# An attention kernel's routing chain: fewer steps for each pair of heads, the written order kept to the last pair, the lists made after it

## The chip, the cores and the metric

One core of a Trainium2 chip runs the whole program. The metric is the device time of one execution in microseconds (us). The engines are named as in the profile: PE (TensorE, matmuls), PEld (its weight loads), DVE (VectorE), ACT (ScalarE), POOL (GpSimd), SP (the queue that issues most DMAs).

## The reference

```python
# attention: B=2, H=8, S=768, D=64, 4 sink keys, window 128
scores = np.where(is_sink | in_window, (q @ k.T) / 8, -1e9)
a = softmax(scores);  x = (a @ v)            # x: 1536 tokens x 512
# first mixture: 8 experts, the best 2 of each token
logits = x @ w_gate;  ns = np.log1p(np.exp(x @ w_noise))
top2 = the two largest of (logits + ns * noise); w = softmax of these two
out[token] += w[k] * (relu(x @ w1[e]) @ w2[e])      # F = 1024
# second mixture: 8 other experts, the best one of each token, gates by softmax
```

## The kernel before

**Attention.** The 1536 tokens are 12 tiles of 128 (`t` = 0 to 11); tiles 0 to 5 are the first batch, 6 to 11 the second. A unit of work is a pair of heads of one tile; there are 48 pairs, and `for j in range(END)` (line 1040) walks over them and 9 steps beyond, which drain what is in flight. In step `j`, pair `j` gets its scores on PE (`s_mm`, line 406: 12 matmuls, or 6 in the first tile of a batch), pair `j-1` its maxima on DVE (`maxima`, lines 412 and 417), pair `j-2` its exponentials on ACT (line 425), pair `j-3` its transposes on PE (line 431), and pair `j-7` its product with v on PE (`pv`, line 461, f32). The scores have two PSUM buffers (`s`). Finished tiles are normalised (`fin_x`, line 537), split into two f16 halves (`x_split`, `x_low`), written to `xrow` in DRAM, turned (`x_turn`), and multiplied with the gate's weights (`lg_mm`, line 568). For tile 5, the last of the first group, `x_turn` is eight PE transposes into a buffer of `s` and one ACT copy (lines 562 and 563), in step 37 together with its `lg_mm`; the logits are ready in step 38.

**The two groups and the gate's chain.** `cuts` puts tiles 0 to 5 in group 0 and 6 to 11 in group 1. When the last logits of a group are there, `gate_ops` makes a list of some 70 small operations, nearly all on DVE (line 609 is the helper that issues them): the noise scale, the best two experts, their counts (PE, lines 647 to 650), ranks, then `lo` and `ct`, the two big comparisons of 128x1536 and 128x1152 elements, the product `ct * tok1`, the matmuls `place` that put the tokens in lists (line 702), and for group 0 `ahead`, which gathers the rows of the first 128 tokens of experts 0 and 1 (POOL, line 936) and queues `ahead_steps`: both layers of these two blocks (lines 894, 799, 817, 909), 28 jobs of PE work that run before group 1's list is known.

**What sets the order.** The list is dripped into the program between other work: `DR` operations after each of the three DVE steps of `maxima`, one after each of the two of `fin_x`, and `TI` at the end of a step (`TD` from step 48 on). A `BAR` in the list lets nothing pass until the end of the step:

```python
def tick(n):
    drip(n)
    for c in chains:
        if c and c[0] is BAR:
            c.pop(0)
```

Up to step `MC` each engine runs its instructions in the order in which they are written (`tc.manual_schedule`). From there on a planner orders them by its own costs, with the written order as priority, except POOL's last part and the last stage. With `MC` 29, steps 29 to 47 of the pairs are the planner's. With `DR` 3 and `TI` 20 group 0's list stands in steps 38 to 47: 29 operations in step 39, `lo`, `ct` and the product in 45, `place` in 46, the gather in 47. Steps 50 and later each issue a job, if there is one.

**After it.** While jobs or lists are left, a loop issues one job and four list operations per turn; group 1's list begins at step 62. Then the rest of experts 0 and 1, experts 2 to 7, and the second mixture follow. The second mixture's routing and experts aren't touched.

The weights of each expert come as f32 and are split into two f16 halves by ACT (line 115, and 111 where POOL makes the low half) and DVE or POOL (lines 122, 120), at written steps as well.

Of the kernel before, what the change touches and what calls it, by code (L numbers as in the profile page):

```python
# [1 line left out]
PRM = {"cuts": [0, 6, 12], "CP": 0, "BARS": 1, "DR": 3, "TI": 20, "TD": 30, "GW": 4, "JB": 50, "JN": 1, "TK": 4,  # L2
# [3 lines left out]
       "JP": 0, "XP": 0, "ptev": 5, "parts": 6, "max": 1, "finx": 10, "ptmm": 3, "exps": 2, "finsum": 9, "pv": 7,  # L6
# [33 lines left out]
def attention_moe_moe(ctx, tc, qk, v, n_sink, window, small, w1, w2, modality_id, modality_bias, w1b, w2b, out, CAP=416):  # L40
# [25 lines left out]

    cuts = PRM['cuts']
    AHEAD = 2
# [271 lines left out]
    def split(t):  # L340
        QZ[t] = qz[t % 3]
        KH[t] = khz[t % 4]
        if t < PRM['direct']:

# [6 lines left out]
        for z, o in ((0, QH[t]), (1, KH[t])):  # L351
            if PRM['qb' if z == 0 else 'kb'] >> t & 1:
                V.tensor_copy(o[:, 0], QK[t][:, z])
# [3 lines left out]
    def split_low(t, x=None):  # L357
        if t < PRM['direct']:
            for y in range(2):
                r = slice(y * D, y * D + D)  # L360
                (G if y else V).tensor_tensor(QZ[t][r, 1, y], QK[t][r, 0], QZ[t][r, 0, y], op=OP.subtract)
        elif not x:
            (V if t == 1 or PRM['ql'] >> t & 1 else G).tensor_tensor(QH[t][:, 1], QK[t][:, 0], QH[t][:, 0], op=OP.subtract)
            for y in range(2):
                r = slice(y * D, y * D + D)
                S.dma_start(QZ[t][r, :, y], QH[t][r])
        if x != 0:
            (G if PRM['kl'] >> t & 1 else V).tensor_tensor(KH[t][:, 1], QK[t][:, 1], KH[t][:, 0], op=OP.subtract)

# [204 lines left out]
    def gate_ops(gi, ts, l):  # L574
# [31 lines left out]
        def op(f, *a, **kw):  # L606
            def run():
                with tc.high_priority(offset=CP):
                    f(*a, **kw)  # L609
            ops.append(run)  # L610

        def bar(k_=1):
            if BARS:
                ops.extend([BAR] * k_)
# [77 lines left out]
        def each(x, m):  # L692
            return x.rearrange("p c k -> p (c k)")[:, None, :].to_broadcast([128, m, 2 * n])

        op(V.tensor_tensor, lo, steps2[:, :, 0:2 * n], each(rh[:, 0], 128), op=OP.is_equal)
        op(V.tensor_tensor, ct, steps2[:, 0:NCOL, 0:2 * n], each(rh[:, 1], NCOL), op=OP.is_equal)
        op(V.tensor_tensor, ct, ct, each(tok1[:, t0:t0 + n], NCOL), op=OP.mult)
        bar()

# [229 lines left out]
    CP = PRM['CP']  # L929
    BARS = PRM['BARS']  # L930
    DR, TI = PRM['DR'], PRM['TI']
# [16 lines left out]
    groups = [list(range(a, b)) for a, b in zip(cuts, cuts[1:])]  # L948

    ends = [ts[-1] for ts in groups]  # L950
    for gi, ts in enumerate(groups):
        for c, t in enumerate(ts):
            def lg(t, c, ts, gi):
                if c == 0:
                    LG[gi] = gk.tile([128, len(ts), 2 * E], FT, name=f"lg{gi}", bufs=1)
                lg_ev(t, LG[gi], c)
                if c == len(ts) - 1:
                    gate_ops(gi, ts, LG[gi][:, 0:len(ts)])
            put(4 * t + (PRM['lge'] if t in ends else PRM['lg']), lg, t, c, ts, gi)
# [68 lines left out]
    JN = PRM['JN']  # L1028
# [10 lines left out]
    MC = PRM['MC']  # L1039
# [345 lines left out]
    TK = PRM['TK']  # L1385
# [349 lines left out]
```

## Time and profile before

| what | us |
|---|---|
| median of 3 runs | 638.49 |
| the three runs | 632.25, 640.03, 638.49 |
| profiled execution, its own time | 641.03 |
| span of the profiled execution | 639.3 |
| mean granted clock over the span | 0.936 of full speed |

The profiled execution is the one that all rows below come from. A granted clock of 0.50 is TensorE at 1.2 GHz, one of 1.00 is 2.4 GHz. In the rows, PE's busy time counts a matmul as long as the profile thinks that it ran, so a PE that is busy all the time at 0.50 does half of what it would do at 1.00.

### The profile page before, as it was taken

Reading aid. Unit: us, or ns where it says so; the run is one execution under the profiler, and the core shown is the slowest. Engines: PE = TensorE matmul, PEld = TensorE weight load, DVE = VectorE, ACT = ScalarE, POOL = GpSimd, SP = SyncE. Lnnn points to the kernel's source line nnn. Section 1 sums busy time; section 2 is a strip of 40 time slices with the busy share of each in tenths; the row PEclk is TensorE's granted clock in tenths of the full one; section 3 lists DMA queues with packets and bytes.
Section 4 is the critical chain, followed back from the end, with each engine's and each line's share of the span. In section 5 each row is a group of like instructions: output and inputs, shape, how many; then the busy total and the mean of one; then the engine's idle time right before and its main releaser. Section 6 shows DMA issues by size and latency. Waiting matters only on the chain. (4 is left out here: it accounts for less than half of the span.)

```text
span 639.3 us, 13126 instructions
## 1 busy us (share of the span) xinstructions
PE 584.5 (91%) x4764; PEld 407.5 (64%) x4764; DVE 378.7 (59%) x1036; ACT 301.8 (47%) x656; POOL 247.3 (39%) x274
## 2 busy tenths in 40 slices
PE   5699989799989999999999999999999697989982
PEld 4699888688867765555555555555545573755761
DVE  8799957934835848464747563356686572473420
ACT  6469857743234847454647463233452341452210
POOL 6577754432141354243341606042312381262210
PEclk9789968857899999999999999999999899889988
DMA  6778975447028578477584506017619865489320
GB/s 211 226 227 218 268 213 149 102 133 246 19 81 210 207 237 261 124 248 175 177 247 166 124 3 154 9 59 277 194 69 338 249 157 134 149 275 215 105 66 9
DMA packets 101048, 107.61 MB, mean 168 GB/s; under 512 B 62579, under 2 KB 65939, under 8 KB 100950
## 3 DMA queue, kind: packets, MB, share of 16 engines
q1 hardware_dynamic: 90102, 76.06, 42.9%
q0 software_dynamic: 9792, 28.26, 13.1%
q10 hardware_dynamic: 1056, 2.10, 0.9%
q8 instruction: 47, 0.77, 0.5%
q14 instruction: 51, 0.42, 0.2%
HBM read 76.03 MB, written 14.74 MB: 142 GB/s over the span
## 5 line engine op out<-in xcount | busy, mean ns | idle before, releaser
L799 PEld LDWEIGHTS <-w1s 128*128 128x128 f16 x1632 | 149.5, 102 | 85.6 <-issue 17.3
L799 PE MATMUL pp<-xtt,w1s 128*128 128x416 f16 (+2 forms) x864 | 152.3, 332 | 1.8 <-issue 1.0
L817 PE MATMUL pp<-hh,w2s 128*128 128x416 f16 (+2 forms) x960 | 141.4, 307 | 0.7 <-DVE hh L802 0.6
L817 PEld LDWEIGHTS <-w2s 128*128 128x128 f16 x960 | 87.7, 99 | 50.1 <-issue 1.0
L751 POOL DMA_INDIRECT yrow<-xga,ids x34 | 36.7, 1079 | 123.7 <-ACT xga L876 118.7
L825 DVE SCALAR_TENSOR_TENSOR yt<-pp,yt 64x416 f16<-64x416 f32 (+1 forms) x64 | 35.5, 555 | 65.2 <-ACT yt L823 58.4
L801 ACT ACTIVATE hh<-pp 128x416 f16<-128x416 f32 (+3 forms) x87 | 38.5, 461 | 57.8 <-PE pp L799 50.5
L802 DVE SCALAR_TENSOR_TENSOR hh<-pp,hh 128x416 f16<-128x416 f32 (+3 forms) x87 | 44.4, 518 | 32.3 <-ACT hh L801 22.7
L823 ACT ACTIVATE yt<-pp 64x416 f16<-64x416 f32 (+1 forms) x64 | 31.0, 485 | 68.1 <-PE pp L817 61.4
L122 DVE SCALAR_TENSOR_TENSOR w1s<-wf,w1s 128x1024 f16<-128x1024 f32 (+1 forms) x49 | 54.3, 1119 | 13.5 <-ACT w1s L115 10.0
L1539 PEld LDWEIGHTS <-hh 128*128 128x128 f16 x336 | 32.6, 98 | 37.9
L122 DVE SCALAR_TENSOR_TENSOR w2s<-wf,w2s 128x1024 f16<-128x1024 f32 (+1 forms) x43 | 52.6, 1262 | 3.3 <-ACT w2s L115 2.8
L461 PE MATMUL po<-vf,ptm 128*128 128x65 f32 x320 | 53.1, 319 | 0.6 <-issue 0.4
L1539 PE MATMUL po<-w2s,hh 128*128 128x512 f16 x240 | 52.8, 379 | 0.0
L461 PEld LDWEIGHTS po<-vf,ptm 128*128 128x128 f32 x320 | 51.2, 241 | 1.9 <-issue 1.2
L115 ACT ACTIVATE w1s<-wf 128x1024 f16<-128x1024 f32 (+1 forms) x51 | 45.6, 924 | 10.6 <-DMA wf<-in_moe_w_dram 5.0
L406 PEld LDWEIGHTS <-w2s 128*128 128x128 f16 x528 | 39.2, 113 | 14.2 <-issue 6.0
L115 ACT ACTIVATE w2s<-wf 128x1024 f16<-128x1024 f32 (+1 forms) x52 | 46.4, 918 | 0.9 <-remote 0.6
L763 POOL DMA_INDIRECT xg<-xrow,idg x30 | 30.2, 1008 | 29.0 <-DVE dst L609 20.1
L802 DVE SCALAR_TENSOR_TENSOR hh<-ph,hh 128x256 f16<-128x256 f32 (+1 forms) x48 | 17.2, 377 | 38.7 <-ACT hh L801 35.8
L406 PE MATMUL s<-w1s,w2s 128*128 128x128 f16 x264 | 31.4, 258 | 7.7 <-DVE w1s L348 5.4
L801 ACT ACTIVATE hh<-ph 128x256 f16<-128x256 f32 (+1 forms) x48 | 15.7, 347 | 46.7 <-PE ph L799 43.4
(304 smaller groups left out, 832.2 us busy)
## 6 DMA issues: line engine op xcount, KB each, us to landing
wf<-in_moe_w_dram SPq DMA_DIRECT2D x44, 1024.0 KB
w1s<-in_qk_dram SPq DMA_DIRECT2D x12, 512.0 KB
vf<-in_v_dram SPq DMA_DIRECT2D x12, 260.0 KB
xrow<-xr SPq DMA_DIRECT2D x12, 256.0 KB
w2s<-xga SPq DMA_DIRECT2D x22, 128.0 KB
wf<-in_moe_w_dram ACTq DMA_DIRECT2D x2, 1024.0 KB
yrow<-xga,ids POOLq DMA_INDIRECT x34
xtt<-xg SPq DMA_TRANSPOSE x31
```

What stands on the lines that cost most here:

```text
L115: A.activation(t[:, 0][:, o[0], o[1]], i, AF.Copy, scale=1.0 if v else SW)
L122: V.scalar_tensor_tensor(t[:, 1][:, o[0], o[1]], i, SW, h, op0=OP.mult, op1=OP.subtract)
L406: T.matmul(PS[t, p][:, c, j], head(t, a, 2 * p + j), KH[t - c][:, b, p // 2 * 2 + j], start=(j + a + b + c == 0), stop=(a > 0 and c == n - ...
L461: T.matmul(o[:, 2 * pp + j], x[:, 2 * pp + j], VV[t - c][:, 2 * p + j], start=(pp + j + c == 0), stop=(i == 0 and j + pp == 2), skip_group ...
L751: return G.indirect_dma_start(out=dst, out_offset=bass.IndirectOffsetOnAxis(ap=idx, axis=0), in_=src, in_offset=None, bounds_check=n - 1, ...
L799: ordered(1, T.matmul(p[:, :n], wa[:, a, d, fs], x[:, c * KD + d, r], start=(k_ == 0), stop=(k_ == len(passes) - 1)))
L801: A.activation(hh[:, 0, f, q], p[:, :n], AF.Relu)
L802: V.scalar_tensor_tensor(hh[:, 1, f, q], p[:, :n], 0.0, hh[:, 0, f, q], op0=OP.max, op1=OP.subtract)
L817: ordered(2, T.matmul(p[:, :n], wt[:, a, f, dd], hh[:, c, f, q], start=(k_ == 0), stop=(k_ == len(passes) - 1)))
L823: A.activation(y[s, 2 * d + x, r], p[s, :n], AF.Copy, scale=z)
L825: V.scalar_tensor_tensor(y[hs[1 - x], 2 * d + x, r], p[s, :n], z, y[s, 2 * d + x, r], op0=OP.mult, op1=OP.subtract)
L1539: T.matmul(p[:m], hh[:, c, f, o:o + m], wb[:, a, f], start=(f == 0 and k_ == 0), stop=(f == KF - 1 and k_ == 2))
```

## The change

Five numbers and two lines. `DR` goes from 3 to 1 and `TI` from 20 to 3, so a step takes six operations of the list, or eight where `fin_x` stands in it. `MC` goes from 29 to 48: the written order holds for all pairs. Two `BAR`s are added between `lo`, `ct` and the product, in group 0's list alone. Counted out by these rules, the list then stands so: ACT's four operations in steps 38 and 39; 28 small DVE operations in steps 40 to 43, the 29th in 44; three in 45; the counts in 46; two operations in 47; a total on PE in 48; eleven small ones and a DMA in 49; `lo` in 50, `ct` in 51, the product in 52, `place` in 53, the gather and the rest in 54. Steps 48 and later are the planner's, and the first job can be written in step 55 (the first four are empty).

```diff
-PRM = {"cuts": [0, 6, 12], "CP": 0, "BARS": 1, "DR": 3, "TI": 20, "TD": 30, ...
-       "MC": 29, ...
+PRM = {"cuts": [0, 6, 12], "CP": 0, "BARS": 1, "DR": 1, "TI": 3, "TD": 30, ...
+       "MC": 48, ...
...
         op(V.tensor_tensor, lo, steps2[:, :, 0:2 * n], each(rh[:, 0], 128), op=OP.is_equal)
+        bar(gi < len(groups) - 1)
         op(V.tensor_tensor, ct, steps2[:, 0:NCOL, 0:2 * n], each(rh[:, 1], NCOL), op=OP.is_equal)
+        bar(gi < len(groups) - 1)
         op(V.tensor_tensor, ct, ct, each(tok1[:, t0:t0 + n], NCOL), op=OP.mult)
         bar()
```

## Rows read from the trace of the kernel before

**Rows 1.** The page, 40 equal slices of 16 us, in tenths: PE busy, granted clock.

```profile
PE   5699989799989999999999999999999697989982
...
PEclk9789968857899999999999999999999899889988
```

**Rows 2.** Windows (us): PE, PEld, DVE, ACT, POOL busy (instructions), clock, DMA share, GB/s.

```profile
83.50:100.60 17.10, 17.10 (x146) 15.98 (x143) 7.70 (x34) 8.02 (x25) 6.84 (x9) 0.50 0.65 151
100.60:124.50 23.90, 19.95 (x238) 17.33 (x238) 23.47 (x102) 18.56 (x50) 13.41 (x17) 1.00 0.52 143
124.50:151.80 27.30, 27.30 (x203) 24.78 (x202) 14.57 (x46) 11.74 (x32) 9.82 (x11) 0.50 0.50 143
...
172.20:175.70 3.50, 3.50 (x42) 3.50 (x40) 2.35 (x11) 1.08 (x4) 1.94 (x2) 0.51 0.21 52
```

**Rows 3.** Timeline of PE: start, us, operation, in brackets the wait before it.

```profile
27.86 0.62 PE L431 MATMUL pt<-identf,p 128*128 128x128 f32 x2 [2.38 <-ACT p L425]
...
83.11 0.24 PE L510 MATMUL sink<-ident,sks 128*64 128x128 f16 x1 [1.40 <-POOL sks L503]
...
123.14 2.28 PE L702 MATMUL misc<-ct,lo 128*128 128x96 f16 x12 [2.34 <-DVE ct L609]
```

**Rows 4.** Windows of line 406 alone (scores, 12 matmuls a pair): PE, PEld, clock, DMA.

```profile
42.30:59.50 17.20, 6.68 (x96) 5.86 (x96) 1.00 0.81 231
69.20:97.10 27.90, 9.40 (x108) 8.29 (x108) 0.76 0.85 224
97.10:126.70 29.60, 10.40 (x120) 8.71 (x120) 0.90 0.51 135
```

**Rows 5.** Windows of all engines, as in group 2: pairs 38 to 47, then the drain.

```profile
97.10:126.70 29.60, 25.65 (x294) 22.33 (x294) 27.06 (x120) 23.09 (x65) 14.97 (x20) 0.90 0.51 135
126.70:146.80 20.10, 20.10 (x120) 17.75 (x121) 8.77 (x26) 7.90 (x20) 6.82 (x9) 0.50 0.47 127
```

**Rows 6.** Timelines of PE and ACT around tile 5's turn.

```profile
94.81 1.01 ACT L563 COPY xt<-s 128x1024 f16<-128x1024 f16 x1 [2.58 <-PE s L562]
...
96.30 0.51 PE L568 MATMUL misc<-wg,xt 128*128 128x16 f16 x12
```

**Rows 7.** Windows of line 609 alone (the chain): PE, PEld, DVE, ACT busy (instructions), clock, DMA.

```profile
98.00:115.10 17.10, 0.07 (x1) 0.10 (x1) 9.54 (x41) 0.94 (x5) 0.92 0.50 140
115.10:119.50 4.40, 0.10 (x1) 0.00 (x0) 3.28 (x9) 0.00 (x0) 1.00 0.49 115
119.50:123.00 3.50, 0.00 (x0) 0.00 (x0) 3.40 (x3) 0.00 (x0) 1.00 1.15 299
123.00:128.00 5.00, 0.00 (x0) 0.00 (x0) 1.35 (x8) 0.00 (x0) 0.65 0.05 10
158.00:165.70 7.70, 0.00 (x0) 0.00 (x0) 5.63 (x42) 0.72 (x5) 1.00 0.23 86
165.70:167.30 1.60, 0.00 (x0) 0.00 (x0) 0.86 (x6) 0.00 (x0) 1.00 0.10 14
167.30:169.80 2.50, 0.00 (x0) 0.00 (x0) 2.30 (x3) 0.00 (x0) 1.00 0.11 7
```

**Rows 8.** Timelines of DVE and POOL: a chain operation beside a weight split.

```profile
105.30 1.16 DVE L609 SCALAR_TENSOR_TENSOR gw<-gw 128x48 f32<-128x48 f32 x1
...
105.06 1.33 POOL L120 TENSOR_TENSOR w1s<-wf,w1s 128x512 f16<-128x512 f32 x1
```

**Rows 9.** Timelines of POOL and PE: second gather, first turn, first and last job's neighbours.

```profile
127.87 0.96 POOL L936 DMA_INDIRECT xga<-xrow,idga  x1 [0.30 <-issue]
...
136.40 0.93 PE L894 MATMUL s<-ident,xga 128*128 128x128 f16 x7
...
146.77 1.46 PE L799 MATMUL s<-xta,w1s 128*128 128x128 f16 x12
...
185.45 4.82 PE L799 MATMUL pp<-xtt,w1s 128*128 128x288 f16 x38 [0.63 <-ACT xtt L784]
```

**Rows 10.** Windows of line 115 alone (weight splits): ACT busy, clock, DMA.

```profile
97.10:126.70 29.60, 8.67 (x15) 0.90 0.51 135
```

More of the change, by code (lines that the diff above doesn't have):

```diff
@@ L1 @@
 import math
-PRM = {"cuts": [0, 6, 12], "CP": 0, "BARS": 1, "DR": 3, "TI": 20, "TD": 30, "GW": 4, "JB": 50, "JN": 1, "TK": 4,
[1 row of a table removed]
+PRM = {"cuts": [0, 6, 12], "CP": 0, "BARS": 1, "DR": 1, "TI": 3, "TD": 30, "GW": 4, "JB": 50, "JN": 1, "TK": 4,
[1 row of a table added]
        1, "direct": 1, "OT": 2, "S3": 0, "SK": 1, "SL": 0, "LS": 2, "L0": 2, "LN": 3, "LW": 12, "EN": 9, "xs": 128,
```

2 rows, old and new, of the table PRM are left out of this document.

## The prediction

> **What bounds the kernel now.** I began with two rows of the page [rows 1]: the granted clock sags in slices 1 to 10, the attention and what follows it, and then stays at 9 for 20 slices, 320 us, in which PE is busy in tenths of 9 as well. So the change, which touches steps 29 to 57 of the attention, is to be read ahead of these slices; and what it wins reaches the end, because PE is the bound of the long stage after it, which only starts earlier or later.
>
> The second view is the windows cut at the clock's own edges [rows 2]. Between 83.5 and 100.6 us, and again between 124.5 and 151.8, PE is busy for the whole of the stretch at 0.50, that is at 1.2 GHz. Between them it runs at 2.4 GHz, has 4 us of idle time in 23.9, and DVE is busy for 23.47. So there are two regimes: PE at half rate, and DVE with the chain.
>
> The third view is PE's timeline ahead of each fall [rows 3]. Falls of the clock come right after a wait of PE: 2.38 us (27.86), 1.40 us (83.11) and 2.34 us (123.14). The last is the chain's own: `lo`, `ct` and the product stand in one row on DVE for 3.4 us [rows 7], the maxima of pair 46 queue behind them, and PE, whose next work needs these maxima or the lists, has nothing. At 151.8 it rose again, after 5 us of the first jobs' f16 matmuls [rows 9]. The planner's order made both of the later waits: at 83.11 it had put a transpose ahead of the next pair's scores, and POOL's operand was late.
>
> The fourth view is the pace of the pairs [rows 4]. In written order and at full clock 96 score matmuls, 8 pairs, take 17.20 us: 2.15 us a pair. The planner's pairs 29 to 37 take 27.9 us (3.10 each, mean clock 0.76), and pairs 38 to 47, with the chain, 29.6 us.
>
> **The change part by part.** I work against the profiled execution (641.03 us, span 639.3); the median of the runs is 2.5 us under it, and the runs spread over 8 us, so I take that difference into the range and not into the sum.
>
> *Pairs 29 to 37, written order.* Nine pairs at 2.15 are 19.4 us. One wait comes with it. In step 37 tile 5's turn and its product with the gate's weights are written one right after the other, and PE may not pass on: the ACT copy between them takes 1.01 us [rows 6]. Before, the planner put transposes and products of other pairs into that gap (1.5 us from the copy's start to line 568). In written order PE waits 1.0 us at least, up to 2.4 if one weight split and a pair of exponentials stand ahead of the copy in ACT's queue; I take 1.2, because a step's exponentials come before it. Behind the waiting matmul stand the scores of pair 38, and behind these DVE. That wait is nearly that of 83.11, so the clock may fall there. The shortest half-rate stretch, 3.5 us [rows 2], costs 1.75 at most; the one of 17.1 us costs 8.5 at most. I take the short one, since only one wait of this length comes, and keep the other for the range. So 19.4 + 1.2 + 1.75 = 22.4 against 27.9: **5.5 us** gained, ends 7.3 and -1.2.
>
> *Pairs 38 to 47, the chain spread.* DVE was busy for 27.06 us there [rows 5]. Out of these pairs go `lo`, `ct` and the product (3.40), the nine operations before them (3.28) and what stood of the last ones (some 0.9) [rows 7]. That leaves 19.5 us, and one more weight split (0.7), 20.2. PE had 25.65, less 2.28 for `place` [rows 3] and less half of the 5.7 us at half rate at the two ends: 20.5, or 2.05 a pair. Neither fills more than ten pairs of 2.15 (21.5 us). The load isn't even, though: 34 of the 41 instructions of the chain's first part fall in pairs 40 to 43 (28 operations, of which six, the indices of the best, are two instructions each). At group 0's price of 9.54 for 41 that is 1.98 a pair, at group 1's 5.63 it is 1.17 [rows 7]. The rest of DVE's work is (20.2 - 9.5) / 10 = 1.07 a pair. So such a pair takes 3.05 or 2.24 in place of 2.15, over four pairs 3.6 or 0.4 us more; I take 2, between them, because POOL's neighbours are group 0's but fewer. 21.5 + 2 = 23.5 against 29.6: **6.1 us** gained, ends 4.5 and 7.7.
>
> The price of 9.54 has a cause in the rows: a 128x48 operation that mostly takes 0.2 us lasted 1.16 and ended with a POOL split that ran at the same time [rows 8]. The Trainium skill, page "SBUF — State Buffer", section "Who interferes with whom", says that a DVE operation with two SBUF inputs and a POOL operation that reads SBUF exclude each other for the whole instruction, and this speaks against spreading: each lone operation may then hold up the maxima behind it. By that rule alone the sum would take the upper price, 1.6 us less gain.
>
> *The drain, with the places in it.* From the last scores' end (126.70) to the first job (146.77) it took 20.1 us, with PE busy throughout at half rate [rows 5, 9]. The same work at full clock is 10.05, and `place` comes to it: 12.3. The chain may be later than that. After pair 47's scores: the eleven small ones 1.6 to 4.4 us, `lo` to the product 2.5 to 3.5 [rows 7], `place` 2.28, the first of the last operations 0.6, two gathers 2.5, the turn 0.5 at full clock and its copy 1.0 [rows 6, 9]; in sum 11.0 to 14.8. The landing of the gathered rows isn't seen: PE turned them 7.6 us after the second issue (127.87 + 0.96 to 136.40) but was busy till then. So it lies between nothing and 7.6; I take 2, near the low end, as full PE explains the rest. The first job then starts 13 to 17 us after the scores, 22.4 at the worst. I take 15 and add 2 for PE's wait in front of it: the clock is likely to fall in it, and `place` itself is thin (at 172.2 the clock fell right after group 1's [rows 2]). 17 against 20.1: **3 us** gained, ends 7 and -2.3.
>
> *What costs nothing.* Weight splits: the planner had pulled 15 of line 115 into pairs 38 to 47 [rows 10]; the written steps hold 7. The other eight, 0.58 us each, fall into the drain, where ACT is busy for 7.9 of 20.1 us and DVE for 8.8 [rows 5]. Without that cover expert 1's first job would be late by up to 4.6 us, but eight jobs of expert 0 stand before it. The gate column's DMA and the two gathers move with the list past SP's and POOL's queues: nothing on these is read by PE before the first job. The two bars themselves fall after step 48, where only priorities are left of the order. From the first job to the rest of expert 0 it took 38.7 us (146.77 to 185.45 [rows 9]), with PE working most of the time; I leave that as it is.
>
> Sum: 5.5 + 6.1 + 3 = 14.6, and 641.0 - 14.6 = 626.
>
> **The rivals.** *The half rate stays.* The wait of step 37 brings a long half-rate stretch, and the drain runs at half rate too. For: 1.40 us was enough at 83.11, and then the clock stayed down for 17.1 us; the drain has no score matmuls. Against: at 172.2 it was back after 3.5 us [rows 2], and from 42.3 to 59.5 written order held it at 1.00 [rows 4]. Then the gains are -1.2, 6.1 and 0: 636.
>
> *The clock never falls.* The wait of step 37 passes and the drain stays at full rate: 7.3 + 6.1 + 7 = 20.4, so 620.6.
>
> *Slower: written order at half rate.* If waits at fixed places hold the clock down through pairs 29 to 47, PE needs some 3.1 us a pair (half of the pairs at 2.05, half at 4.1): 58.9 us for 19 against 57.5. Then the drain's 20.1 us of PE come with 2.2 more for `place`, and if the lists end only after it, gathers, landing, turn and copy (6 us) follow openly: 28.3 against 20.1. That is 9.6 lost: 650.6. It decides from a pace of 2.6 us a pair on, where 19 pairs win just the 8.2 us that the drain loses.
>
> *It doesn't do what it says.* In the drain the planner may draw the chain's operations forward or behind as it likes, so that "one a pair" is only a priority; and if tile 5's logits come late, the list slips. Then only the order of pairs 29 to 37 is changed, and the clock decides: 638.
>
> **How the numbers follow.** The forecast case (621.5 to 631) has 0.47, the half rate that stays (631 to 638) 0.25, the clock that never falls (below 621.5) 0.15, slower 0.07, no effect 0.06. Two per cent, about what a measurement of this kernel tells from no change, is 625.7 and 651.3 from the median. Faster than that is the full-clock case, and a good half of the forecast's, as the median lies 2.5 under the profiled time: 0.42. Slower by 2% is half of the slower case with some room for the unseen landing: 0.05. Same: 0.53. The range leaves out the fastest of the full-clock cases and the slower one: 617 to 638.
>
> **What would show it.** Right: 2.1 to 2.3 us a pair from 29 to 37; no wait of 2 us around the comparisons before the last scores; last scores near 114 us; first job near 131; `place` after the last scores with other PE work beside it. A wait of line 568 on the ACT copy of 1 to 1.5 us shows the price of written order. Wrong: a clock at 0.50 through pairs 38 to 47, PE idle for more than 4 us ahead of the first job, or a first-layer start of expert 0's rest (185.45 before) that moved by much less than the first job, because group 1's chain and not PE sets it.

## The result, and the profile after

The change made the kernel a little slower: a median of 641.98 us over 20 runs (637.35 to 653.20) against 638.20 over 20 runs of the kernel before. The ratio is **1.0085**, 95% interval 1.0058 to 1.0112. Ratios here leave out executions that took over 1.5% longer than the fastest of their kernel, while medians and means use all. The forecast was 626 us, the upper end of its range 638.

The profiled execution after took 640.69 us, its span is 638.9. It stands 1.3 us under its median, while the one of before stood 2.8 us above the median of 638.20, so the two profiles end level although the medians don't. In the code of after, lines behind 697 are three higher: 702 is 705, 799 is 802, 894 is 897, 936 is 939.

The page's slices of PE and granted clock, which answer to [rows 1]:

```profile
PE   5699898878889989999899999999999788978982
...
PEclk9799889958999999999999999999999799899998
```

Windows of line 406 alone (columns as in [rows 4]), pairs 29 to 37 and pairs 38 to 47:

```profile
67.80:93.00 25.20, 9.09 (x108) 7.97 (x108) 0.86 0.95 245
93.00:118.40 25.40, 9.05 (x120) 7.76 (x120) 0.93 0.55 160
```

The 19 pairs take 50.6 us against 57.5 [rows 4]. That is a gain of 6.9, where 11.6 was forecast, but pairs 29 to 37 are far from 2.15 us each: 2.80. Windows of all engines from the last scores on, which answer to [rows 5]: up to the fall of the clock, at half rate, the whole drain, the early jobs of experts 0 and 1, their rest, and what follows from expert 2 on:

```profile
118.40:127.50 9.10, 7.14 (x75) 5.84 (x74) 8.96 (x32) 7.98 (x25) 8.76 (x10) 1.00 0.82 251
127.50:147.90 20.40, 16.43 (x118) 13.85 (x118) 6.18 (x20) 4.05 (x10) 7.85 (x6) 0.50 0.66 171
...
118.40:145.30 26.90, 20.98 (x167) 17.09 (x167) 15.14 (x50) 12.03 (x33) 16.61 (x16) 0.67 0.72 195
145.30:182.80 37.50, 31.25 (x498) 28.24 (x497) 19.10 (x99) 12.79 (x44) 4.90 (x5) 0.96 0.17 51
182.80:234.70 51.90, 49.36 (x409) 38.17 (x409) 28.06 (x58) 25.03 (x47) 21.38 (x21) 1.00 0.74 215
234.70:638.90 404.20, 371.42 (x2516) 220.78 (x2513) 216.64 (x440) 168.67 (x293) 129.13 (x116) 0.98 0.55 158
```

The drain takes 26.9 us where it took 20.1, with 5.9 us in which PE is idle (26.90 - 20.98; before none). So the 6.9 us are gone at the first job: 145.27 against 146.77 [rows 9]. Timeline of PE, the waits that count (columns as in [rows 3]):

```profile
76.79 0.48 PE L568 MATMUL misc<-wg,xt 128*128 128x16 f16 x12 [2.81 <-DMA xt<-xr]
...
92.42 0.46 PE L568 MATMUL misc<-wg,xt 128*128 128x16 f16 x12 [1.22 <-ACT xt L563]
...
127.19 1.70 PE L461 MATMUL po<-vf,ptm 128*128 128x65 f32 x8 [1.94 <-ACT w2s L115]
...
129.06 4.53 PE L461 MATMUL po<-vf,ptm 128*128 128x65 f32 x20
133.39 0.70 PE L705 MATMUL misc<-ct,lo 128*128 128x96 f16 x3
...
142.39 1.03 PE L897 MATMUL pp<-ident,xga 128*128 128x128 f16 x8 [2.87 <-DMA xga<-xrow,idga]
...
145.27 2.02 PE L802 MATMUL pp<-xta,w1s 128*128 128x128 f16 x17
...
182.76 9.47 PE L802 MATMUL pp<-xtt,w1s 128*128 128x288 f16 x76 [0.63 <-ACT xtt L787]
```

The wait at 92.42 is the forecast one, tile 5's turn in step 37. The one at 76.79 was not forecast: the same line in step 31, for a tile that a DMA turns. The granted clock falls with each of the two, at 76.3 for 6.8 us and at 93.3 for 3.4 us (windows of all engines):

```profile
76.30:83.10 6.80, 6.31 (x68) 6.32 (x69) 3.19 (x14) 5.26 (x16) 4.45 (x5) 0.50 1.06 342
...
93.30:96.70 3.40, 3.40 (x27) 3.40 (x25) 1.16 (x6) 3.31 (x14) 3.32 (x5) 0.50 0.51 131
```

The long wait ahead of `place` [rows 3] is gone. A new one stands at the gathered rows, because the places now come after the scores. DVE's timeline shows the chain there:

```profile
122.88 0.68 DVE L609 TENSOR_TENSOR ow<-oh,wv 128x96 f32<-128x96 f32 x1
...
127.44 0.72 DVE L609 TENSOR_TENSOR ct<-steps,rh 128x1152 f16<-128x1152 f16 x1
...
129.29 0.73 DVE L609 TENSOR_TENSOR ct<-ct,tok 128x1152 f16<-128x1152 f16 x1
...
138.01 0.26 DVE L609 TENSOR_TENSOR lst<-misc,lst 128x96 f32<-128x96 f32 x1 [2.04 <-PE misc L705]
```

### The profile page after: what moved, and what is told of

Read it like the earlier page. It is cut to its first block, busy times and chain, and to the rows that moved or that the text cites. A ratio compares the mean times of both kernels' runs of the same rounds, so it can differ in the third digit from the quotient of the medians.

```text
span 638.9 us, 13134 instructions
## 1 busy us (share of the span) xinstructions
PE 570.8 (89%) x4764; PEld 394.0 (62%) x4764; DVE 376.3 (59%) x1036; ACT 302.6 (47%) x656; POOL 246.8 (39%) x274
## 2 busy tenths in 40 slices
DMA packets 101048, 107.61 MB, mean 168 GB/s; under 512 B 62579, under 2 KB 65939, under 8 KB 100950
## 5 line engine op out<-in xcount | busy, mean ns | idle before, releaser
L802 PEld LDWEIGHTS <-w1s 128*128 128x128 f16 x1632 | 147.2, 101 | 88.2 <-issue 20.8
L820 PEld LDWEIGHTS <-w2s 128*128 128x128 f16 x960 | 85.9, 98 | 52.1 <-issue 3.1
L122 DVE SCALAR_TENSOR_TENSOR w1s<-wf,w1s 128x1024 f16<-128x1024 f32 (+1 forms) x49 | 56.1, 1156 | 16.2 <-PE pp L802 7.4
L461 PE MATMUL po<-vf,ptm 128*128 128x65 f32 x320 | 44.6, 287 | 2.0 <-ACT w2s L115 1.9
L406 PEld LDWEIGHTS <-w2s 128*128 128x128 f16 x528 | 37.3, 110 | 13.9 <-issue 6.2
L461 PEld LDWEIGHTS po<-vf,ptm 128*128 128x128 f32 x320 | 43.1, 209 | 2.4 <-POOL sks L503 2.0
L766 POOL DMA_INDIRECT xg<-xrow,idg x30 | 29.4, 980 | 31.5 <-DVE dst L609 22.6
```

Of the source, the lines that this page charges most:

```text
L122: V.scalar_tensor_tensor(t[:, 1][:, o[0], o[1]], i, SW, h, op0=OP.mult, op1=OP.subtract)
L406: T.matmul(PS[t, p][:, c, j], head(t, a, 2 * p + j), KH[t - c][:, b, p // 2 * 2 + j], start=(j + a + b + c == 0), stop=(a > 0 and c == n - ...
L461: T.matmul(o[:, 2 * pp + j], x[:, 2 * pp + j], VV[t - c][:, 2 * p + j], start=(pp + j + c == 0), stop=(i == 0 and j + pp == 2), skip_group ...
L802: ordered(1, T.matmul(p[:, :n], wa[:, a, d, fs], x[:, c * KD + d, r], start=(k_ == 0), stop=(k_ == len(passes) - 1)))
L820: ordered(2, T.matmul(p[:, :n], wt[:, a, f, dd], hh[:, c, f, q], start=(k_ == 0), stop=(k_ == len(passes) - 1)))
```

## The experiments

Each run of a kernel has a span and a mean granted clock. As the clock has two levels, 2 x (1 - clock) x span is its time at half rate. Over 94 runs of before (its 20 runs above have no clock on record) and 155 of the others, with a constant for each kernel, the time rises by 0.36 us (standard error 0.014) for each us at half rate. The last column is what a kernel costs against before at equal half-rate time, with its 95% interval; s.e. is the standard error. These two columns are worked out, not measured.

| kernel | median us (runs) | ratio to before, 95% | mean us at half rate (s.e.) | at equal half rate |
|---|---|---|---|---|
| before | 638.9 (94) | 1 | 73.8 (1.0) | 0 |
| the change | 642.0 (20), 641.4 (13) | 1.0085 [1.0058, 1.0112], 1.0071 [1.0037, 1.0105] | 73.9 (2.5) | +3.1 ± 0.9 |
| order_only | 651.9 (6) | 1.0236 [1.0183, 1.0289] | 101.4 (2.0) | +1.8 ± 2.0 |
| drip_only | 638.6 (6) | none | 65.6 (5.5) | +0.9 ± 1.9 |
| bars_only | 637.9 (12) | 1.0002 [0.9954, 1.0051] | 66.5 (2.1) | +1.2 ± 1.4 |
| drip_bars, drip_bars_2 | 637.4 (12), 636.0 (12) | 0.9967 [0.9918, 1.0015], 0.9934 [0.9886, 0.9982] | 62.4 (1.8) | +1.8 ± 1.4, +1.1 ± 1.4 |
| order_drip | 639.9 (12) | 1.0058 [1.0022, 1.0094] | 73.0 (3.6) | +1.4 ± 1.4 |
| written_37 | 638.4 (13) | 0.9962 [0.9922, 1.0002] | 63.1 (2.9) | +3.1 ± 1.3 |
| written_38_47 | 636.3 (12) | 0.9976 [0.9939, 1.0013] | 65.3 (3.9) | +0.4 ± 1.4 |
| lg_later | 638.4 (13) | 1.0018 [0.9986, 1.0049] | 68.5 (2.7) | +1.4 ± 1.3 |
| lg_all_later | 636.0 (12) | 0.9983 [0.9950, 1.0017] | 65.6 (1.3) | -0.3 ± 1.4 |
| splits_later | 642.3 (12) | 1.0088 [1.0049, 1.0128] | 70.4 (2.4) | +4.3 ± 1.4 |

**The change once more, and each of its parts alone.** The change is three numbers (`DR`, `TI` and `MC`, not five) and two bars. The first run is the changed kernel as it is.

> The changed kernel once more, for a second profile and a comparison on the same chip. In the first profile the last scores began 7.7 us sooner than before (117.5 against 125.2), the first job only 1.5 sooner (145.3 against 146.8). Drain theory: that repeats; wait of PE for ACT and DVE in the drain, clock at 0.50 from about 127 to 148, ratio 1.005 to 1.012. Luck theory (the clock falls elsewhere from run to run): last scores or first job differ by more than 4 us between the two profiles, ratio within 0.998 to 1.004.

It gave 641.35 us, a ratio of 1.0071: the loss repeats, as the drain theory had it. Its profile, of an execution of 653.01 us, doesn't: the first job came at 160.23 and not at 145.27, so one of the luck theory's two signs is there as well.

Written order to the last pair, on the kernel before:

```diff
-       "MC": 29,
+       "MC": 48,
```

> Written order to step 47, with the old drip: 29 chain operations in step 39, the comparisons in 45, the gather in 47. Drain theory (written order moves weight splits into the drain, where they hold up the pairs' ends and the lists): as slow as the change, 640 to 644, first job at 143 to 148, though last scores come before 123. Late-list theory (what costs is that the gather was moved from step 47 to 54): faster than before, at most 636, since the gather is early and the order written.

Windows of all engines over pairs 29 to 37 and pairs 38 to 47:

```profile
73.80:100.20 26.40, 21.52 (x272) 19.93 (x271) 18.57 (x75) 21.11 (x56) 14.36 (x17) 0.86 0.90 233
100.20:137.80 37.60, 35.74 (x291) 32.45 (x288) 25.72 (x117) 19.97 (x59) 17.98 (x20) 0.60 0.41 114
```

The ratio is 1.0236, the worst of all, and both expectations missed. PE is busy for 35.74 of 37.6 us in the ten pairs, at a mean clock of 0.60. This is the pace of the rival "written order at half rate", and more; its long drain is not there (20.8 us, from 137.79 to 158.56).

The thin list alone, and the two bars alone, on the kernel before:

```diff
-"DR": 3, "TI": 20
+"DR": 1, "TI": 3
```

> The planner's order from step 29 as before, but the thin drip of the change, without the two bars. Drain theory: no difference, 636 to 640, since the planner still pulls weight splits into the pairs and chain operations to where they are ready. Late-list theory: 641 to 645, with the gather written 6 steps later, and the first job later than 148.

```diff
+        bar(gi < len(groups) - 1)
         op(V.tensor_tensor, ct, steps2[:, 0:NCOL, 0:2 * n], each(rh[:, 1], NCOL), op=OP.is_equal)
+        bar(gi < len(groups) - 1)
```

> The two bars alone, on the kernel before: ct written in step 46, its product in 47, the places in 48, the gather in 49. Drain theory: 636 to 640, the wait of 2.3 us ahead of the places shorter or gone. Late-list theory: 639 to 642, by two steps of about 2.9 us of which part is hidden.

Neither can be told from no change (for the first there is no ratio). In the thin one's profile the planner's pairs 38 to 47 run at full clock, at 2.15 us each. Windows of line 406 over pairs 29 to 37 and 38 to 47:

```profile
69.50:92.60 23.10, 8.17 (x109) 7.05 (x108) 0.94 0.95 260
92.60:114.10 21.50, 8.49 (x120) 7.18 (x120) 1.00 0.55 155
```

So the loss needs the written order, and the planner's own pace in pairs 29 to 37 is 23.1 us here (21.8 with the bars), not the 27.9 of the profile before.

**The written order taken out of the change, or halved.** First the change with the planner from pair 29 on, then the same kernel again.

```diff
-       "MC": 48,
+       "MC": 29,
```

> The change without its written order: thin drip and two bars, the planner's order from step 29. Theory of the waits (in written order PE stands at steps 31, 35 and 37 for tiles that are turned by a DMA or copied by ACT: 2.8, 1.4 and 1.2 us in the profiles): no such waits, 636 to 640. Theory of the drain (the late gather costs): as slow as the change, 641 to 644, the first job 24 us or more after the last scores.

> The thin list and the bars with the planner's order in pairs 29 to 47 once more, to narrow 0.997 (0.992 to 1.0015). Theory (the thin list wins a little in the pairs and loses it in the drain, with nothing over): 0.997 to 1.002. Rival (the shorter pairs are a real gain of 2 us or more): 0.992 to 0.997, with an interval below 1.

The ratios are 0.9967 and 0.9934, the second with an interval below 1: the rival of the second expectation, a real gain of a few us. This version beats both kernels: on the mean over all its runs it is 2.7 us (95% interval ± 2.0) under before. Windows of the second one, line 406, and PE's timeline in its drain:

```profile
72.80:95.90 23.10, 8.14 (x109) 7.04 (x108) 0.94 0.98 258
95.90:117.40 21.50, 8.49 (x120) 7.14 (x120) 1.00 0.54 151
```

```profile
140.37 1.03 PE L897 MATMUL pp<-ident,xga 128*128 128x128 f16 x8 [3.08 <-DMA xga<-xrow,idga]
```

The pairs are short and the drain is as long as in the change: 25.8 us from the last scores (117.33) to the first job (143.17), with the wait for the gathered rows in it. So the long drain comes with the late lists, not with the written order.

Then the written order to pair 37 only, and in pairs 38 to 47 only.

```diff
-       "MC": 48,
+       "MC": 38,
```

> The change with the planner's order from step 38 on. Theory of the waits: they all lie before 38 and stay, 640 to 643; pairs 29 to 37 take 25 us or more. Theory of the drain: from step 38 on the planner pulls the weight splits and the chain forward again, so 636 to 639, first job within 24 us of the last scores.

```diff
-        if j == MC:
+        if j in (MC, 48):
             man.close()
+        if j == 38:
+            man.enter_context(tc.manual_schedule(engines=MS | {ET.SP}))
```

(with `MC` 29)

> The change, but with the planner's order back in pairs 29 to 37; pairs 38 to 47 keep the written order. Theory (the waits of written order at fixed places in steps 31, 35 and 37, some 5 us in all, are the loss): they are gone, so ratio to before 0.995 to 1.003, pairs 29 to 37 in 22 to 23 us, like with the planner in all pairs. Rival (written order is dear in pairs 38 to 47, where the chain's operations, the exponentials and the splits meet): ratio 1.006 to 1.010, as with the whole change. Rival (only the two together are dear, each half alone is nothing that can be measured): 0.995 to 1.002, which with written order to pair 37 alone at 0.996 would leave no price for either half.

Windows of line 406, pairs 29 to 37, of the first and of the second:

```profile
70.50:95.30 24.80, 8.93 (x108) 7.84 (x108) 0.86 0.95 251
```

```profile
68.60:87.70 19.10, 7.32 (x111) 6.40 (x110) 1.00 1.05 290
```

Ratios of 0.9962 and 0.9976: neither half of the written order costs what the whole does. For the first half the theory of the waits had expected 640 to 643 and missed, and the drain theory had the time right but not the first job, which came 27.7 us behind the last scores. The second ratio fits the theory of the waits and that of the two halves together alike, with pairs 29 to 37 even below the 22 us expected. The table splits it in part. At equal half-rate time written order in pairs 29 to 37 costs 3.1 us against before, and 1.7 ± 1.5 against the same kernel with the planner throughout (drip_bars, 1.4 on the mean of its two sets). Its profile has the wait of step 31 (2.71 us) and none at line 568 in steps 35 and 37. But it spends 63 us at half rate, not 74, which pays for that. Written order in pairs 38 to 47 costs nothing in the whole time that can be measured. In the pairs themselves it does: they took 29.3 us in its profile, with waits of PE for DVE of 1.62 and 1.04 us, and 24.3 at a clock of 1.00 in the profile of splits_later (below), where the planner with the thin list took 21.5 at 1.00. Windows of line 406, pairs 38 to 47, of these two:

```profile
87.70:117.00 29.30, 10.04 (x120) 8.53 (x120) 0.83 0.65 172
```

```profile
97.30:121.60 24.30, 8.35 (x120) 7.05 (x120) 1.00 0.47 126
```

**The waits at line 568 taken away.** The change, with the products of the DMA-turned tiles one step later, and then with tile 5's too (which puts the chain one step later).

```diff
-"lgmm": 19, ... "lg": 20,
+"lgmm": 20, ... "lg": 21,
```

> The change with the gate's product of a tile (and the reading of it) written one step later, except for the last tile of a group. Theory of the waits: the waits at steps 31 and 35 fall from 2.8 and 1.4 us to under 1 and nothing, pairs 29 to 37 take 22.5 us in place of 25 to 26.5, and the time is 637 to 639.5. Theory of the drain: these waits are covered by the drain's own, 641 to 644.

```diff
-"lgmm": 19, "lgmme": 17, "lg": 20, "lge": 18,
+"lgmm": 20, "lgmme": 18, "lg": 21, "lge": 19,
```

> The change, with every product with the gate's weights (line 568) one step later, tile 5's too, which brings the chain one step later as well. Theory (waits at lines 568): no wait over 1 us in steps 31, 35 and 37; with the first two gone the ratio was 1.002, so 0.998 to 1.003 here. Rival (the list is late in the drain, and a step later costs more): first job 1 to 2.5 us further behind the last scores than the 27 of the change, ratio 1.003 to 1.010.

Windows of line 406 in the second, pairs 29 to 37 and pairs 38 to 47:

```profile
69.70:89.10 19.40, 7.49 (x108) 6.38 (x109) 1.00 1.07 296
89.10:119.10 30.00, 10.25 (x120) 8.86 (x120) 0.83 0.58 149
```

The first move leaves waits of 0.91, 0.50 and 1.10 us at line 568. With both moves PE waits nowhere there, and nine written pairs take 19.4 us at a clock of 1.00. The ratio falls from 1.0085 and 1.0071 to 1.0018 and then 0.9983, as the theory of the waits had it; the first job came 25.3 us behind the last scores (144.32 - 119.05), no later than in the change. On the mean over all runs it is 6.3 us faster than the change (636.6 against 642.9): 8.3 us less at half rate make 3.0 of that, 3.3 are left at equal half rate. The profiles don't show how these reach the end. In this one the next ten pairs give back 4.6 of the 5.8 us that the first nine won, with two waits of PE for DVE (2.23 us at 102.68, 2.38 at 107.61) and 10.3 us at half rate. From pair 29 to the first job it takes 74.6 us, the change's profile 77.5; the rest of the difference between the two profiles lies behind the first job.

**Two other suspects in the drain.** Three weight splits in later steps, away from the drain's start; and the change without its bars.

```diff
-"wh": [..., 52, 55, 61]
+"wh": [..., 60, 62, 66]
```

> The change with the last three pieces of expert 1's weight splits written in steps 60 to 74, behind the first group's gather, in place of 52 to 67. Theory of the drain (splits on ACT and DVE in it hold up the pairs' ends and the lists): the wait for ACT of 1.9 us in the drain goes, the first job comes within 24 us of the last scores (27 to 30 in the change), 637 to 640. Theory of the waits: 641 to 643, since pairs 29 to 37 keep theirs.

```diff
-        bar(gi < len(groups) - 1)
         op(V.tensor_tensor, ct, steps2[:, 0:NCOL, 0:2 * n], each(rh[:, 1], NCOL), op=OP.is_equal)
-        bar(gi < len(groups) - 1)
```

> The change without its two added bars: lo, ct and the product stand in one step of the drain. Theory (in the drain the bars only space out what the planner may order, and the written order is the loss): ratio 1.006 to 1.011, and last scores to first job 24 to 27 us. Rival (the bars put the lists three steps later and this is what the drain loses): first job 20 to 22 us behind the last scores and a ratio of 0.998 to 1.003.

Later splits change nothing: 1.0088, and the first job is 27.0 us behind the last scores (148.60 - 121.59). PE's wait of 1.9 us in the drain stays as well (1.93, now put down to DVE), so the splits' place is not the loss.

Without the bars the drain is shorter, 22.6 us (142.72 - 120.14), between the two expectations. The ratio is 1.0058, and its interval reaches both the rival's 1.003 and the change's. So what the bars do to the whole time isn't settled: 1.4 ± 1.4 us at equal half-rate time, where the change has 3.1 ± 0.9. In these two profiles, though, they are 4.3 of the 6.8 us by which the drain grew. The product of `ct` ends 11.3 us behind the last scores without them and 11.7 with them. Then `place` (line 703 here) starts 1.1 us later, in place of 3.4, and runs in one stretch, where the change's is cut up by other matmuls:

```profile
132.51 2.29 PE L703 MATMUL misc<-ct,lo 128*128 128x96 f16 x12
```

The two bars write `place` two steps later, behind 12 more matmuls of line 461; the planner takes the written order as priority.

## Why the prediction was wrong

**Two steps of the sum failed.** By size the first is the drain: 17 us forecast, 26.9 measured, which is 9.8 of the 14.5 us that the three terms fell short. The one that made a loss of it is the price of the written order in pairs 29 to 37: "One wait comes with it", set against the planner's 27.9 us. Both sides of that difference were off.

- *The wait counted was right, two others were not seen.* Step 37's wait was forecast at 1.2 us and measured 1.22; 3.4 us at half rate follow it, as forecast. But line 568 also stands at a fixed place in steps 31 and 35, for tiles that a DMA transposes. In the profile before these steps are the planner's, and PE shows no wait at that line; in written order PE waited 2.81 and 0.21 us in steps 31 and 35 of the change's profile, and 2.51 and 1.44 in its second one. In all six profiles that have the wait of step 31 (2.40 to 2.81 us) the clock falls with it, for 3.4 or 6.8 us. I had counted only the turn on ACT. Nine pairs at 2.15, 19.4 us, is exact as soon as the waits are gone and the clock stays at 1.00: lg_all_later took 19.4. Tile 3's transpose was issued two steps ahead, from 66.59 on, and PE had its result at 76.79. SP needed 2.83 and 5.03 us to issue it and the next one, 1.53 to 1.59 for the three before; the DMA share of these pairs is 0.95 in the row above, but that this is the reason isn't shown. Timeline of SP, the turns of tiles 2, 3 and 4:

```profile
57.12 1.53 SPq L558 DMA_TRANSPOSE xt<-xr  x1
...
66.59 2.83 SPq L558 DMA_TRANSPOSE xt<-xr  x1
...
75.81 5.03 SPq L558 DMA_TRANSPOSE xt<-xr  x1
```

- *The planner's 27.9 us were one execution's.* They hold the 17.1 us at half rate from 83.5 on [rows 2]. In five other profiles with the planner in these pairs they took 23.1, 21.8, 21.8, 23.1 and 19.1 us. Against those the written order of the change (25.2) loses 2 to 6 us in place of winning 5.5. The fall at 83.5 was taken to follow from the wait of 1.40 us at 83.11. Four of the five have the same wait at the same line, and in none of them does the clock fall there. PE's timeline and the next 17 us of all engines, from drip_only:

```profile
84.77 0.24 PE L510 MATMUL sink<-ident,sks 128*64 128x128 f16 x1 [1.40 <-POOL sks L503]
```

```profile
84.80:101.80 17.00, 17.00 (x236) 15.87 (x236) 14.74 (x58) 13.64 (x43) 11.61 (x15) 1.00 0.67 195
```

**Pairs 38 to 47**, forecast 23.5 us: the change's profile has 25.4 (29.6 before), a gain of 4.2, just under the lower end of 4.5. The term itself was right about the thin list and needs no written order: under the planner at full clock the ten pairs took 21.5 in three profiles. At the place where a rule was weighed, the upper price came true: 39 instructions of line 609 on DVE took 8.81 us between 95.0 and 118.4, 0.226 each, nearly group 0's 0.233 [rows 7]:

```profile
95.00:118.40 23.40, 0.00 (x0) 0.00 (x0) 8.81 (x39) 1.03 (x5) 0.96 0.59 173
```

Spreading didn't make them cheaper. That is the side on which the Trainium skill, page "SBUF — State Buffer", section "Who interferes with whom", stood. The trace agrees: an operation on 1x2 elements, 0.14 us long at 116.69 in the profile before, lasts 1.15 us in the drain and ends with the POOL operation beside it. Timelines of DVE and POOL:

```profile
124.04 1.15 DVE L609 SCALAR_TENSOR_TENSOR acum<-bump,acum 1x2 f16<-1x2 f32 x1
...
124.03 1.15 POOL L551 TENSOR_TENSOR xr<-x,xr 128x512 f16<-128x512 f32 x1
```

The price didn't set the pace, though: with the planner 40 such instructions took 10.29 us (drip_bars_2, 95.9 to 117.4), and the ten pairs still 21.5.

**The drain**, forecast 17 us, a gain of 3: it took 26.9, a loss of 6.8. By the timeline after, from the last scores' end at 118.36: DVE, busy for 8.96 of 9.10 us, does one of the eleven small operations at 120.63 and comes to the other ten only at 122.88 (4.5 us, which I had at nothing); these take to 127.44 (4.6, forecast 1.6 to 4.4); `lo` to the product ends at 130.02 (2.6, as forecast); `place` starts 3.4 us behind that, after 20 matmuls of line 461 at half rate, and takes to 137.97 in between other work, 4.6 for 2.28. The gathers take 2.5, as forecast; the rows are turned 1.1 us after the second, where I had 2; the turn to the first job takes 2.9, for 1.5. Lateness of DVE, and PE's own queue at half rate, were the missing 10 us. In the second the bars have a part, which stood under what costs nothing: without them `place` ends 14.7 us behind the last scores and not 19.6 (order_drip). But the drain is not what makes the change slower than before: it is 25.8 us in drip_bars_2, which is faster.

**From the first job on.** "Left as it is" held: 35.9 to 39.8 us from the first job to the rest of expert 0 in all 14 profiles. That a gain there reaches the end held too, within some us: the rest began between 175.8 and 197.8, and from there to the end it took 451.2 to 459.8. That spread is larger than the loss, so no two profiles can show where the loss sits. In the change's own profile 2.7 us were lost again between 182.8 and 234.7 (51.9 for 49.2 us), where PE is idle for 2.5 of them, so that expert 2 starts at 234.69 in both kernels.

**The rivals.** "Slower: written order at half rate" had 0.07. It was to decide from 2.6 us a pair on; the change's 19 pairs take 2.66 (50.6 / 19), and win just what the drain loses, 6.9 and 6.8. Without the thin list (order_only) its number came, 651.9 us with 650.6 forecast, but by other terms: 64.0 us for the 19 pairs and 20.8 for the drain, where it had 58.9 and 28.3. "The half rate stays" was right on the drain, which is at half rate for 17.8 of its 26.9 us. "It doesn't do what it says" was right in one thing: in the drain the bars spaced nothing out, `lo`, `ct` and the product stood within 2.6 us. One of the signs listed as wrong was there: PE idle for more than 4 us in the drain, 2.87 of them right ahead of the first turn.

**The cause**, then. The thin list, with the bars, is worth some 2 to 4 us, in less time at half rate (62 us against 74). The written order over all pairs takes that back and costs 3 us more on the mean (642.9 against 639.8), and all of it goes away when line 568 stands one step later (lg_all_later). So that line's place is shown to be the cause of the loss for the whole change. Two things stay open. One is how the waits' us reach the end, as the profiles above don't show it. The other is why written_37, which has the wait of step 31 and the fall of the clock with it, spends 63.1 us at half rate and the change 73.9, which is 10.8 us apart with a standard error of 3.8.

## What to carry to other kernels

Before a stretch is handed from a planner to the written order, list each instruction of the bound engine in it that reads another queue's result, DMAs too, and ask how many steps lie between issue and landing; one step more for each took 6.3 us off the mean here. Don't price the planner by one profile in which the clock fell: take the pace of the stretch from several executions, or at equal clock. When work is moved behind the last cover, count from when its engine is free, not from when its input is there. And a bar that only changes the priority of what follows it can still put that behind other work.

## What the runs showed of the hardware

A stretch at 0.50 can outlast everything near its start, with PE busy for all of its first half. In lg_later a wait of PE of 1.10 us ended at 89.82, and the clock stayed at 1.2 GHz from 90.1 to 158.4 us; after the wait of 1.22 us in the change it stayed there for 3.4 us. Windows of all engines over pairs 38 to 47 and the drain:

```profile
90.40:126.80 36.40, 36.40 (x280) 33.28 (x277) 22.60 (x102) 19.98 (x60) 18.84 (x23) 0.50 0.45 117
126.80:157.00 30.20, 25.69 (x167) 21.71 (x167) 13.71 (x50) 10.07 (x28) 11.88 (x14) 0.50 0.57 167
```

How much time goes at half rate differs from run to run of one kernel: before's runs scatter by 9.9 us (standard deviation) around 74 us. An us at half rate cost 0.36 us and not 0.5. Why isn't shown; in the change's drain PE is idle for 4.0 of the 20.4 us at 0.50. The same program's profiles differ by several us, and a single one can hide a loss of 0.85%.
